# A fused S4 + gated-FFN training step on one core: skip products as diagonal matmuls, more buffers in the transform stages, and stores queued one step later

## The chip, the core and the metric

The kernel runs on one core of one Trainium2 chip. Its time is the device time of an execution in microseconds (us). Six executions had a median of 1852.91 us (1845.04 to 1858.05). Within a core, five engines each work through a queue of their own: TensorE (PE in the profile; its weight loads are PEld), VectorE (DVE), ScalarE (ACT), GpSimd (POOL) and SyncE (SP), which issues most DMA transfers.

Each experiment was timed in five rounds against the kernel before, on the same chip. A ratio is the mean time of one kernel's fast runs over that of the other's of the same rounds, so it is not quite the ratio of the medians that I quote beside it.

## The reference, cut to what matters

The program computes the output of a block and its gradients. `x` is layer-normed to `xn`; an S4 branch (a long convolution done with FFTs, plus a per-channel skip) and a gated feed-forward branch are added; then all is differentiated.

```python
xn = _layernorm(x)
out = x + _A_ref(xn, ...) + _B_ref(xn, ...)
# in _A_ref:   y = irfft(rfft(u) * rfft(K))[:L] + u * Dskip      # u is xn, Dskip has one value per channel
# in _B_ref:   h = relu(x @ W_gate) * (x @ W_up);  return h @ W_down
_out, _vjp = jax.vjp(_f, ...);  grads = _vjp(grad_out)            # L = 2048, D = 576, F = 4608, N = 128
```

So two products with `Dskip` are needed at the very end: `xn * Dskip` for the output, and `grad_out * Dskip` for the gradient that flows back into the layer norm.

## The kernel before

The feed-forward branch goes through F in 12 chunks (0 to 11). Per chunk, an `a_unit` makes hidden activations, `outdx` makes output and input gradient for one tile of 128 rows (summed over chunks in DRAM, `acc_dram`, by a DMA that adds), and `dw_down`, `dw_gu` and `dw_left` make the weight gradients. The S4 branch is interleaved with this: forward transform (`p1`), kernel stage (`p2`), last transform (`p3`), twice, for the two halves of the channels. In chunk 11 the 16 row tiles are finished by `Final`: its terms are added into the same PSUM sum, and VectorE and ScalarE do the rest.

```python
    def fwd1(self, hf, ns, load, ap, n, gap):                 # first step of a transform
        for n2 in range(ST):
            ...
            A = ap.tile([P, 2, ns, DH], BF16, name=f"fA{ns}")     # same pool as the loaded tiles
            ...                                                  # matmul into PSUM, copy into A
            nc.sync.dma_start(self.A[ns][hf][:, n2], A[:])

    def p3(self, hf, n, gap):                                 # second step of the last transform
            fp = self.pool(c, f"p3_f{hf}", 2, "right")
            zp = self.pool(c, f"p3_z{hf}", 3, "right")
            for h in range(ST + 1):
                old, Z = Z, None
                if h < ST:
                    ...                                          # mix: 4 small matmuls, 2 copies
                    Z = self.product(zp, pp, sg[:, 0], sk[:], False), self.product(zp, pp, sg[:, 1], sk[:], True)
                if old is not None:
                    for i in range(2):
                        Ct = fp.tile([P, 2, 1, DH], BF16, name="fC2")
                        yield from self.unmix(Ct[:, :, 0, :], old[i])
                        nc.sync.dma_start(self.mix_in(self.C[2][hf], h - 1)[:, :, i:i + 1, :], Ct[:])

class Final:
    def load(self, t):                                        # two row tiles ahead
        ...
        base = self.pool.tile([P, 2, D], F32, name="f_base")     # self.pool has 3 buffers
        nc.vector.tensor_tensor(base[:], xg[:], self.dsk[:].unsqueeze(1).to_broadcast([P, 2, D]), op=ALU.mult)
    def take(self, t, i, cols, ps):                           # four times per row tile
        base = self.parts[t][5]
        dst = self.o[:, 0, cols] if i == 0 else base[:, 1, cols]
        self.g.nc.vector.tensor_tensor(dst, base[:, i, cols], ps, op=ALU.add)
```

Output tiles of the feed-forward branch, `osx`, have three buffers.

## Time and profile before

The first line of the profile page, busy time, share of the span and number of instructions of each engine:

```profile
PE 1741.8 (94%) x16257; PEld 1179.5 (64%) x16257; DVE 1379.2 (75%) x3223; ACT 1173.7 (63%) x2647; POOL 206.0 (11%) x246
```

PE is the engine to watch: 108 us of the span of 1850.2 are idle on it. The table of stretches (start:end, length, then busy time and instructions of PE, PEld, DVE, ACT, POOL; at the end PE's granted clock, DMA share, GB/s) says where:

```profile
core 0: us, PE busy (x) PEld busy (x) DVE busy (x) ACT busy (x) POOL busy (x), PEclk, DMA share, GB/s
90.00:300.00 210.00, 189.78 (x1450) 119.47 (x1449) 146.64 (x337) 141.50 (x321) 19.16 (x28) 0.95 0.91 291
...
1530.00:1620.00 90.00, 74.77 (x507) 40.96 (x504) 77.87 (x254) 62.79 (x168) 6.90 (x8) 0.96 0.85 236
1620.00:1697.00 77.00, 74.33 (x630) 50.86 (x628) 16.75 (x37) 24.17 (x55) 6.90 (x8) 1.00 0.68 190
1697.00:1812.00 115.00, 102.27 (x801) 71.88 (x799) 93.84 (x208) 49.60 (x96) 0.00 (x0) 0.99 0.68 210
```

In the last transform (1530 to 1620) DVE is busy for 77.87 us beside PE's 74.77; in the final rows (1697 to 1812) it is busy for 93.84 of 115. In the final rows DVE's groups of instructions (line, operation, output<-inputs, shape, count | busy us, mean ns | idle time before them, and what ended it) begin with these:

```profile
L1024 DVE TENSOR_TENSOR f_base<-f_xg,dsk 128x1152 f32<-128x1152 bf16 x13 | 17.6, 1357 | 12.7 <-DMA f_xg<-in_grad_out_dram 12.6
L1043 DVE TENSOR_TENSOR f_base<-f_base,ps_mm 128x288 f32<-128x288 f32 x32 | 14.0, 449 | 3.4 <-PE ps_mm L290 3.4
L1043 DVE TENSOR_TENSOR f_o<-f_base,ps_mm 128x288 bf16<-128x288 f32 x32 | 13.9, 447 | 1.5 <-PE ps_mm L290 1.5
```

The base product costs 1.36 us of work, and DVE also stands idle for 12.7 us in front of it, since it waits for a load. From the list of waits of the whole run (waiter <- releaser: us in total, times, longest):

```profile
PE ps_mm L290 <- ACT osx L67: 14.3, 24, 2.2
...
DVE exs L567 <- DMA ex_dram<-exs: 11.9, 5, 5.4
...
ACT osx L67 <- DMA acc_dram<-osx: 8.4, 4, 3.2
...
DVE osx L61 <- DMA acc_dram<-osx: 3.9, 1, 3.9
```

### The profile page before, as it was taken

Reading aid. Unit: us, or ns where it says so; the run is one execution under the profiler, and the core shown is the slowest. Engines: PE = TensorE matmul, PEld = TensorE weight load, DVE = VectorE, ACT = ScalarE, POOL = GpSimd, SP = SyncE. Lnnn points to the kernel's source line nnn. Section 1 sums busy time; section 2 is a strip of 40 time slices with the busy share of each in tenths; the row PEclk is TensorE's granted clock in tenths of the full one; section 3 lists DMA queues with packets and bytes.
Section 4 is the critical chain, followed back from the end, with each engine's and each line's share of the span. In section 5 each row is a group of like instructions: output and inputs, shape, how many; then the busy total and the mean of one; then the engine's idle time right before and its main releaser. Section 6 shows DMA issues by size and latency. Waiting matters only on the chain. (4 is left out here: it accounts for less than half of the span.)

```text
span 1850.2 us, 41883 instructions
## 1 busy us (share of the span) xinstructions
PE 1741.8 (94%) x16257; PEld 1179.5 (64%) x16257; DVE 1379.2 (75%) x3223; ACT 1173.7 (63%) x2647; POOL 206.0 (11%) x246
## 2 busy tenths in 40 slices
PE   7989989999999999999999999999999998899988
PEld 5655547667566666766666766766766754476656
DVE  7565975686898787787887889889888747923872
ACT  5865855686587488477487567657748736733432
POOL 0200002112012012002102101102201100010000
PEclk9989999999999999999999999999999999999999
DMA  8798988668557566776676856856754879785763
GB/s 285 264 325 292 331 243 264 196 172 232 177 125 203 181 183 168 211 186 146 197 203 137 231 157 154 237 159 122 196 177 93 187 230 259 215 220 163 250 196 100
DMA packets 236411, 373.26 MB, mean 202 GB/s; under 512 B 49202, under 2 KB 153140, under 8 KB 234676
## 3 DMA queue, kind: packets, MB, share of 16 engines
q1 hardware_dynamic: 210244, 304.08, 50.6%
q0 software_dynamic: 24384, 51.92, 18.5%
q10 hardware_dynamic: 1584, 14.60, 2.3%
q8 instruction: 127, 2.08, 0.4%
q14 instruction: 72, 0.59, 0.1%
HBM read 233.08 MB, written 137.43 MB: 200 GB/s over the span
## 5 line engine op out<-in xcount | busy, mean ns | idle before, releaser
L67 ACT CAST osx<-ps_mm 128x288 bf16<-128x288 f32 x684 | 262.0, 422 | 72.7 <-PE ps_mm L290 61.6
L303 POOL DMA_DIRECT2D acc_dram<-osx x160 | 139.4, 875 | 1039.2 <-ACT osx L67 582.2
L290 PE MATMUL ps_mm<-wf,dgT 128*128 128x288 bf16 x1152 | 208.9, 288 | 17.0 <-ACT osx L67 11.9
L343 PEld LDWEIGHTS <-rows 128*128 128x128 bf16 x1536 | 146.0, 98 | 97.5 <-issue 4.6
L290 PE MATMUL ps_mm<-wf,duT 128*128 128x288 bf16 x1152 | 207.0, 288 | 0.0
L290 PE MATMUL ps_mm<-wf,hT 128*128 128x288 bf16 x1152 | 186.4, 289 | 7.7 <-ACT osx L67 2.4
L235 PE MATMUL ps_mm<-xT,wd_158 128*128 128x512 bf16 x720 | 182.4, 379 | 0.7 <-ACT xT L149 0.7
L235 PE MATMUL ps_mm<-gT,wd_160 128*128 128x512 bf16 x705 | 180.3, 382 | 2.0 <-ACT obw L67 2.0
L235 PE MATMUL ps_mm<-xT,wd_159 128*128 128x512 bf16 x720 | 181.5, 380 | 0.5 <-ACT obw L67 0.5
L245 DVE SCALAR_TENSOR_TENSOR upm<-rg,ps_mm 128x512 bf16<-128x512 bf16 x144 | 98.1, 682 | 99.2 <-PE ps_mm L235 71.3
L327 PE MATMUL ps_mm<-rows,hN 128*128 128x144 bf16 x2304 | 156.8, 227 | 0.0
L327 PEld LDWEIGHTS <-hN 128*128 128x128 bf16 x2304 | 147.7, 98 | 7.7 <-issue 5.2
L290 PEld LDWEIGHTS <-dgT 128*128 128x128 bf16 x1152 | 109.7, 98 | 53.5 <-issue 25.3
L343 PE MATMUL ps_mm<-duN,rows 128*128 128x384 bf16 x768 | 138.6, 326 | 0.0
L343 PE MATMUL ps_mm<-dgN,rows 128*128 128x384 bf16 x768 | 136.6, 326 | 0.1
L290 PEld LDWEIGHTS <-hT 128*128 128x128 bf16 x1152 | 107.6, 98 | 41.8 <-issue 12.5
L290 PEld LDWEIGHTS <-duT 128*128 128x128 bf16 x1152 | 113.0, 98 | 31.7 <-issue 2.2
L67 ACT CAST obw<-ps_mm 128x384 bf16<-128x384 f32 x105 | 50.1, 477 | 125.6 <-PE ps_mm L343 93.9
L67 ACT CAST dhb<-ps_mm 128x512 bf16<-128x512 f32 x141 | 83.8, 594 | 66.6 <-PE ps_mm L235 64.9
L901 DVE TENSOR_REDUCE Sm<-pr 128x8 f32<-128x256 f32 x288 | 119.1, 413 | 3.6
L243 ACT ACTIVATE rg<-ps_mm 128x512 bf16<-128x512 f32 x144 | 86.9, 604 | 54.7 <-PE ps_mm L235 53.2
L235 PEld LDWEIGHTS <-wd_159 128*128 128x128 bf16 x720 | 65.6, 98 | 62.5 <-issue 2.7
(2513 smaller groups left out, 3511.4 us busy)
## 6 DMA issues: line engine op xcount, KB each, us to landing
acc_dram<-osx POOLq DMA_DIRECT2D x176, 288.0 KB, 4.7
gT<-in_gT_dram SPq DMA_DIRECT2D x48, 640.0 KB, 6.4
xT<-xT_dram SPq DMA_DIRECT2D x44, 640.0 KB, 6.0
rows<-in_gq_dram SPq DMA_DIRECT2D x48, 576.0 KB, 4.7
wf<-in_Wf_dram ACTq DMA_DIRECT2D x11, 1296.0 KB, 8.7
ex_dram<-exs SPq DMA_DIRECT2D x18, 640.0 KB, 5.8
ex<-ex_dram SPq DMA_DIRECT2D x36, 320.0 KB, 3.3
out_dram<-obw SPq DMA_DIRECT2D x96, 96.0 KB, 2.7
```

The costliest lines, as they stand in the source:

```text
L67: self.nc.scalar.copy(out, in_)
L235: nc.tensor.matmul(ps[:], lhsT=w[:, k, fs], rhs=rhs[:, k, :], start=(k == 0), stop=(k == NK - 1))
L243: nc.scalar.activation(rg[:], ps_g[:], ACT.Relu)
L245: nc.vector.scalar_tensor_tensor(upm[:], rg[:], 0.0, ps_u[:], op0=ALU.is_gt, op1=ALU.mult)
L290: nc.tensor.matmul(ps[:, :DH], lhsT=lt, rhs=rh, start=(i == 0), stop=(i == len(mms) - 1))
L303: nc.gpsimd.dma_start(g.acc_dram[:, t, :, :], o[:], accum_op=ALU.add)
L327: nc.tensor.matmul(ps[:, ft * 144:(ft + 1) * 144], lhsT=self.hN[:, st, ft * P:(ft + 1) * P], rhs=gq[:, st, :], start=(st == 0), stop=(st = ...
L343: nc.tensor.matmul(ps[:, :Fc], lhsT=xs[:, st, 0:P], rhs=src[:, st, :], start=(st == 0), stop=(st == ST - 1))
L901: nc.vector.tensor_reduce(out=Sm[:, vi, s0 + dd:s0 + dd + DG, :], in_=pr[:], op=ALU.add, axis=AX.X)
```

## The change

It intends to take the skip products off VectorE, to let transform steps run further ahead of their stores, and to keep loads from standing in the SP queue behind stores that still wait for data.

```diff
 # 1. Final: skip products on PE. The diagonal 128x128 blocks of Dskip come from the host's layout.
-                    mms = last.terms(t, which, hf) + mms
+                    src0 = self.X[(c, sg)][which]
+                    mms = [... terms ...] + [(src0[:, k, js], last.dsk[:, k, a], b) for k, a, b in last.skip(hf)] + mms
-        base = self.pool.tile([P, 2, D], F32, name="f_base")
-        nc.vector.tensor_tensor(base[:], xg[:], self.dsk[:]...to_broadcast([P, 2, D]), op=ALU.mult)
-        self.g.nc.vector.tensor_tensor(dst, base[:, i, cols], ps, op=ALU.add)
+        if i == 0:
+            self.g.bal.copy(self.o[:, 0, cols], ps, DH)                  # VectorE or ScalarE
+        else:
+            self.g.nc.scalar.activation(self.dx[:, cols], ps, ACT.Copy, accum_out=self.m[:, hf:hf + 1])
 # 2. buffers
-        self.op = pool("ffn_o", 3)
+        self.op = pool("ffn_o", 4)                                       # osx
-            A = ap.tile([P, 2, ns, DH], BF16, name=f"fA{ns}")
+            A = op.tile([P, 2, ns, DH], BF16, name=f"fA{ns}")            # own pool, 2 * n - 2 * (n < 4) buffers
-            fp = self.pool(c, f"p3_f{hf}", 2, "right")                   # the same in p1
-            zp = self.pool(c, f"p3_z{hf}", 3, "right")
+            fp = self.pool(c, f"p3_f{hf}", n, "right")                   # n is 4 for p1(0) and p3(1), else 2
+            zp = self.pool(c, f"p3_z{hf}", n, "right")
 # 3. stores one step later
+class Lag:
+    def put(self, nc, dst, src):
+        self.flush()                                                    # queue the previous store
+        self.q.append((nc, dst, src))
-            nc.sync.dma_start(self.A[ns][hf][:, n2], A[:])
+            lag.put(nc, self.A[ns][hf][:, n2], A[:])                     # also for S and C
 # 4. order in p3: the two products no longer come before the two unmixes
-                    Z = self.product(zp, ...False), self.product(zp, ...True)
+                for i in range(2):
+                    if h > 0:  ... unmix(Z[i]); lag.put(...)
+                    if h < ST: Z[i] = self.product(zp, pp, sg[:, i], sk[:], i == 1)
 # 5. product() uses one scratch tile instead of two; exponent tiles of half the size, 5 buffers instead of 3
-            exp_ = self.pool(c, "par_ex", 3)
+            exp_ = self.pool(c, "par_ex", 5)
```

## The prediction

> **What bounds the kernel.** The matrix engine (PE): the page gives it 1741.8 us busy of a span of 1850.2 (94%); its idle time is 108 us, and removed waits can win no more. The table of stretches puts that at: 13 us in 0-90 (start), 20 in 90-300 (first forward transform beside the parameter stage, clock 0.95), 20 in 300-1000, 17 in 1000-1500, 15 in 1530-1620 (last transform), 13 in 1697-1812 (final outputs), 4.5 in the tail. Two stages have another limit: in 1530-1620 the vector engine (DVE) is busy 77.9 of 90 us; in 1697-1812 it is busy 93.8 of 115 and idles 12.7 more in front of `f_base` (groups of that stretch), mostly for the `f_xg` load.
>
> **Costs and gains by stage.**
> 1. Final outputs. DVE loses 16 `f_base` products of 1.36 us (22 us) and 64 PSUM additions of 0.45 us (29 us). ACT loses 16 copies with sum (0.87 us, 14 us) and gets 32 half-width ones (estimate 0.6 us each, 19 us); 32 PSUM copies of about 0.42 us are shared. PE gains 64 groups of three matmuls. Transposes of 128 columns follow each other every 56 ns (four in 0.22 us in the timeline), so I take 55 ns each, the short ones too: 10.6 us. The Trainium skill ("TensorE: Matmul & The Clock Gate", Back-to-back issue gap) gives about 56 ns as isolated gap and 81 as sustained rate for 128 columns; the trace agrees with the first. All 10.6 us are critical. DVE stops being the limit, PE becomes it: 102.3 us busy now + 10.6 + 2 to 3 idle, against 115. **Net 0 to +2 us**: work moves from an engine that was full to one that then is.
> 2. Last transform. With two buffers ACT waits for `C_ydu` stores to free `fC` (about 11 us in the list of waits) and PE behind it for PSUM (some 10 us). Four buffers and alternating unmix and product remove most. But DVE does the same 73 us of products (0.46 + 2x0.30 + 4x0.30 us, 32 times) and is 87% busy, so less than the idle 15 us comes back: **-8**.
> 3. 90-300. PE waits 7.3 us for `fA` copies, which wait for `A_ug` stores or each other: separate, more buffers remove most, and the clock dips (0.80 in 100-125) go with the gaps. Half-size `exs` tiles cut part of DVE's 12 us of waiting for `ex_dram` stores. The 5.3 us wait for `bC` at the change of phase stays. **-8**.
> 4. Fourth `osx` buffer: PE waits 14.3 us behind ACT's `osx` copies, but only 8.4 + 3.9 us of what holds ACT and DVE there are `acc_dram` stores; the rest is three PSUM buffers. **-4**.
> 5. Late stores. The SP queue's own waits on data to store add up to over 150 us, but PE waits on DMA for about 16 us, 14 of them at start and phase change. Loads are early enough: **-2**.
>
> Sum about -21 us: **1832 us**, 8 in 10 between 1812 and 1850. Faster by over 2%: 0.13; within 2%: 0.85; slower: 0.02.
>
> **What would show it.** PE busy up 10-11 us, PE idle down from 108 to about 77. In the final-output stage PE over 95% busy, DVE under 65%, length within 3 us of before. In the last transform no waits on `C_ydu` stores, DVE over 90% busy. No `fA` waits in 90-300.
>
> **What would make it wrong.** New buffers may change the instruction order on PE, and new in-order stalls may eat the gains (or more idle goes). The short matmuls might cost as much as weight loads (98 ns): +8 us. ACT, with sums in front of PSUM release, might hold PE in the final stage. DVE might not limit the last transform: then -12 there.

## The result, and the profile after

The changed kernel takes 1824.81 us (median of 10 runs, 1821.73 to 1830.56) against 1849.99 us (20 runs). The ratio is 0.986, with a 95% interval of 0.9847 to 0.9874, so about 26 us are gone. The same line of the page, and the first three of the same stretches (fixed times: the last transform's products lie in or close to 1530 to 1620 in both kernels, but the work after it lay up to 28 us later before; the final rows follow below, cut where they begin and end):

```profile
PE 1745.0 (96%) x16449; PEld 1183.9 (65%) x16449; DVE 1353.1 (74%) x3175; ACT 1188.6 (65%) x2716; POOL 205.1 (11%) x246
```

```profile
90.00:300.00 210.00, 191.97 (x1498) 121.44 (x1497) 151.76 (x360) 143.74 (x340) 22.79 (x31) 0.95 0.93 297
...
1530.00:1620.00 90.00, 83.76 (x581) 45.70 (x579) 81.52 (x252) 71.56 (x185) 10.26 (x13) 1.00 0.86 240
1620.00:1697.00 77.00, 77.00 (x685) 54.34 (x683) 22.52 (x50) 24.12 (x56) 2.89 (x4) 1.00 0.64 197
```

PE idle time fell from 108 to 76.5 us (1821.5 - 1745.0), almost exactly as predicted. But 192 matmuls were added, and PE's busy time rose by only 3.2 us. The Trainium skill ("Perfetto Trace Analysis", Identifying the Most-Contended Engine) warns that matmul busy share is not a good measure of how close a kernel is to roofline, because matmuls are pipelined. This trace shows a related fault of it: a matmul of 288 columns is recorded as 0.29 us long but the next one starts 0.12 us later, so every stall adds a piece of pipeline to "busy" and every stall removed takes it away.

So I used another measure, worked out from the trace: the time from the start of one matmul to the start of the next, less the usual spacing for its number of columns (0.0555 us for 128, 0.1215 for 288, 0.2155 for 512, and so on). What remains is time **lost** on PE: waits, and also what a lower granted clock costs. (The measure needs a complete record. These two hold 16257 and 16449 matmuls, as many as the 192 added ask for; those of e1, e2, e4 and e5 lack some 147 each, and I don't use it there.) By this measure the run before lost 141.9 us, the run after 105.2, and the added matmuls cost 8.5 us: 141.9 - 105.2 - 8.5 = 28.2 us, which accounts for the 28.7 us between the two profiled spans.

The stretches below are cut where the work cuts itself, so they hold the same feed-forward work in each kernel. "Rest" is from the first weight gradients of chunk 1 to those of chunk 9, "transform" from there to those of chunk 10, "weights" is the weight-gradient stretch that follows, "final rows" is from the first final row tile to the last weight gradients, and the tail is 40 us in all of them.

```
length in us            start  rest(1-9)  transform  weights  final rows   span of the profiled run
before                  297.4   1177.3     173.6      49.9      111.6      1850.2
after                   293.7   1171.5     160.0      49.9      106.2      1821.5
difference               -3.7     -5.8     -13.6       0.0       -5.4       -28.7
```

The final rows, cut in this way (before, then after, from the table of stretches):

```profile
1698.20:1809.80 111.60, 98.86 (x756) 68.90 (x754) 90.80 (x200) 47.34 (x92) 0.00 (x0) 0.98 0.69 214
1675.10:1781.30 106.20, 104.47 (x948) 76.97 (x946) 57.28 (x135) 59.64 (x147) 0.00 (x0) 1.00 0.76 239
```

VectorE's busy share fell from 81% to 54%, and PE is busy for 98% of the stretch. In it the waits of PE on VectorE, in the kernel before,

```profile
PE pt L264 <- DVE dgT L253: 7.7, 3, 3.6
...
PE ps_mm L290 <- DVE f_o L1043: 3.9, 4, 1.1
```

are gone; what is left in the kernel after is a load:

```profile
PE ps_mm L235 <- DMA gT<-in_gT_dram: 1.5, 2, 1.3
```

PE loses 3.0 us there instead of 16.9. The diagonal matmuls are seen in the timeline of PE (start, duration, instruction, number merged):

```profile
1768.29 0.29 PE L291 MATMUL ps_mm<-f_acc,ident_bf 128*128 128x288 bf16 x1
1768.42 0.29 PE L291 MATMUL ps_mm<-dsk,xT 128*128 128x128 bf16 x3
1768.56 0.53 PE L291 MATMUL ps_mm<-wf,hT 128*128 128x288 bf16 x3
```

The three of them push the next matmul back by 0.14 us (1768.42 to 1768.56), not by their recorded 0.29 us.

The two lists of waits differ in these lines (after):

```profile
DVE exs L582 <- DMA ex_dram<-exs: 16.2, 6, 6.3
...
PE ps_mm L291 <- ACT osx L67: 4.8, 10, 1.5
```

PE's waits behind `osx` copies fell from 14.3 to 4.8 us and no engine waits for an `acc_dram` store any more. The waits on the half-size exponent tiles did not fall. Also no engine waits for a store of the last transform (`C_ydu`), where ACT had waited some 12 us before.

### The profile page after: what moved, and what is told of

Same layout as the page of the kernel before. It is cut to its first block, busy times and chain, and to the rows that moved or that the text cites. A ratio compares the mean times of both kernels' runs of the same rounds, so it can differ in the third digit from the quotient of the medians.

```text
span 1821.5 us, 42302 instructions
## 1 busy us (share of the span) xinstructions
PE 1745.0 (96%) x16449; PEld 1183.9 (65%) x16449; DVE 1353.1 (74%) x3175; ACT 1188.6 (65%) x2716; POOL 205.1 (11%) x246
## 5 line engine op out<-in xcount | busy, mean ns | idle before, releaser
L291 PEld LDWEIGHTS <-hT 128*128 128x128 bf16 x1152 | 104.5, 98 | 37.6 <-issue 7.9
```

Of the source, the lines that this page charges most:

```text
L291: nc.tensor.matmul(ps[:, cs], lhsT=lt, rhs=rh, start=(i == 0), stop=(i == len(mms) - 1))
```

## The experiments

My theory was that the five parts of the change add up, each in its own stretch: buffers give most, the diagonal products a few us in the final rows. The rivals: the late stores do it, or the order in the last transform, or one part is worth something only with another. Twelve kernels ran; all gave correct results. First the sizes, with the profile of each cut as above:

```
                        ratio to before (95%)       start  rest   transf.  weights  final rows
before                  1                           297.4  1177.3  173.6    49.9     111.6
after                   0.9860 (0.9847-0.9874)      293.7  1171.5  160.0    49.9     106.2
one part alone
 e1  final stage only   0.9968 (0.9951-0.9984)      298.0  1176.9  170.2    49.9     105.9
 e5  buffers only       1.0032 (1.0012-1.0052)      295.4  1189.3  163.4    56.4     112.6
 e11 4th osx only       1.0008 (0.9982-1.0034)      298.8  1176.3  161.9    61.5     113.3
 e9  4 final buffers    0.9990 (0.9968-1.0012)      295.6  1177.5  175.7    49.9     108.6
one part undone in after
 e2  stores at once     0.9851 (0.9834-0.9868)      292.2  1171.8  160.9    49.9     106.9
 e3  3 osx buffers      0.9928 (0.9911-0.9946)      293.6  1180.7  165.2    51.7     106.7
 e4  few buffers        0.9888 (0.9869-0.9907)      293.1  1172.4  164.1    49.9     105.4
 e6  old order in p3    0.9893 (0.9875-0.9911)      293.0  1176.9  160.9    49.9     105.9
 e7  big exponent tiles 0.9847 (0.9829-0.9865)      288.0  1175.8  159.8    49.9     106.7
another way for the skip products, on top of after
 e8  folded on DVE      0.9905 (0.9885-0.9925)      293.2  1171.9  159.3    59.2     103.4
 e10 ... 4 buffers      0.9904 (0.9882-0.9927)      295.2  1174.0  159.7    59.6     103.7
 e12 ... mixed          0.9891 (0.9871-0.9911)      290.1  1175.2  159.7    59.0     108.0
```

The stretches are of one profiled run of each kernel, and runs of one kernel differ by several us. The profiled run of e5 took 1859.16 us, while three of its six runs took 1851.6 to 1852.8 and three 1859 to 1861; that of e8 took 1829.09 beside a median of 1834.72; that of e3 is its slowest (1840.53). The ratios tell what a kernel is worth; a difference of two or three us in one stretch is only a hint.

### e1: the final stage alone

Edit: the kernel before, with part 1 of the diff.

> The kernel before with only the new final stage (diagonal products on PE, no base products and additions on DVE). Theory (DVE relief): the stage between the down-weight products of chunk 10 and chunk 11 gets about 5 us shorter as in the changed kernel, all earlier stages stay within 1 to 2 us, so the total is 4 to 7 us lower (about 1844 beside 1850). Rival (the final stage only got shorter because the last transform ended earlier and the loads came earlier): total within 2 us of before, or higher by the 8 us of added matmuls.

Measured: 1843.77 us beside 1850.42. The final rows fell from 111.6 to 105.9 us, as in the changed kernel, with the last transform still at its old place. The rival falls: relief of VectorE in this stretch is worth 5.7 us net of the added matmuls. The transform stretch is 3.4 us shorter too, where I had allowed 1 to 2; the kernel before has its first three base products there, which e1 has not.

### e2: stores at once

```diff
     def put(self, nc, dst, src):
-        self.flush()
-        self.q.append((nc, dst, src))
+        nc.sync.dma_start(dst, src)
```

> The changed kernel with every store queued at once, as before; all buffers as in the changed kernel. Theory (buffers do it, the late stores are worth little): 0 to 3 us slower than the changed kernel. Rival (the late stores do it, since loads no longer stand behind waiting stores in the SP queue): 8 us or more slower.

Measured: 1823.24 us, no slower than the changed kernel. The late stores, one of the three parts in the change's title, are worth nothing measurable here. In the kernel before PE waited on DMA only five times, 16.1 us in all, 14.1 of them at the start and at a change of phase.

### e4: few buffers, with late stores and the new order

```diff
-            fp = self.pool(c, f"p3_f{hf}", n, "right")          # the same in p1
-            zp = self.pool(c, f"p3_z{hf}", n, "right")
+            fp = self.pool(c, f"p3_f{hf}", 2, "right")
+            zp = self.pool(c, f"p3_z{hf}", min(n, 3), "right")
             # fA pools: n buffers instead of 2 * n - 2 * (n < 4)
```

> The changed kernel with the old numbers of buffers in the transform stages (2 for fC, s_k and s_ug, 4 instead of 8 for fA where four loads are ahead), late stores kept. Theory (buffers do it): 9 to 14 us slower than the changed kernel, more than half of it in the chunk with the last transform, and ACT again waits for C_ydu stores there, longer than before since the stores are late. Rival (late stores or the alternating order do it): 0 to 3 us slower.

Measured: 1830.48 us, by the ratios 5 us slower than the changed kernel, 4.1 us of it in the transform stretch. That is between the two expectations: the buffers count for about half of what my theory gave them. The waits of ACT on `C_ydu` stores come back, but as 3.3 us, not as more than before.

### e5: the buffers alone

Edit: part 2 of the diff without the `osx` line (and `zp` at `max(n, 3)`), and part 5's single scratch tile, which made room; everything else as before.

> The kernel before with only the buffers of the transform stages raised (and the second scratch tile of the product dropped, for room); stores at once, old order, three osx buffers, old final stage. Theory (buffers do it): 10 to 14 us faster than before, mostly in the chunk with the last transform, no waits on C_ydu stores. Rival (buffers alone only let the work run ahead until DVE is full, order or late stores are needed): under 5 us faster.

Measured: 1855.98 us, which is **slower** than before by 0.3%. The transform stretch did shrink by 10.2 us and the `C_ydu` waits are gone, just as my theory said. But in the profiled run, one of the slower three, 12 us came back in the middle, and 6.5 us in the weight gradients, a stretch that has no transform work at all. Buffers gave what was expected where they were put, and something else took it away. The second part is explained by e11 below; the first is not (see the end of this section).

### e3: three osx buffers

```diff
-        self.op = pool("ffn_o", 4)
+        self.op = pool("ffn_o", 3)
```

> The changed kernel with three instead of four osx buffers. Theory (the fourth osx buffer removes the waits for acc_dram stores, the longest of them 7 us long right before the weight products of chunk 10): 4 to 8 us slower than the changed kernel. Rival (osx stores are covered anyway, the gain outside the final stage comes from the transform order): within 2 us of the changed kernel.

Measured: 1837.64 us, which by the ratios is 13 us slower than the changed kernel: half of the whole gain, from one digit. 9.2 us are in the middle of the run, 5.2 in the transform stretch. PE's waits behind `osx` copies and the store waits are back, as this list of e3's waits shows:

```profile
PE ps_mm L291 <- ACT osx L67: 11.7, 14, 4.1
...
ACT osx L67 <- DMA acc_dram<-osx: 9.4, 5, 5.4
...
DVE osx L61 <- DMA acc_dram<-osx: 4.6, 1, 4.6
```

### e6: the old order in the last transform

Edit: part 4 of the diff undone, `lag.put` kept.

> The changed kernel with the old order inside the last transform (both products, then both inverse mixes), buffers and late stores as changed. Theory A (the alternating order is what takes the in-order stalls out where the transform runs beside the kernel stage and in the last transform): 6 to 12 us slower than the changed kernel. Theory B (buffers take them out, the order is worth little): 0 to 3 us slower.

Measured: 1829.79 us, by the ratios 6 us slower, at the lower edge of theory A. But the loss is hardly in the last transform (0.9 us). 5.4 us of it are in the middle of the run, and of these only about 1 in the chunks beside which the first half's last transform runs (1010 to 1310 us). The rest comes from stretches in which the edited step hardly runs; that the order of instructions changed there is my guess and not shown. So theory A has its size right but not its place.

### e7: big exponent tiles

Edit: part 5's exponent tiles as before (double size, 3 buffers).

> The changed kernel with the exponent tiles of double size again (three buffers). The prediction credited the half-size tiles with part of the gain before 300 us. Theory now (the waits on ex_dram stores did not fall, 16 us after against 12 before, so they gave nothing): within 2 us of the changed kernel. Rival: 3 us or more slower, all of it by the second chunk.

Measured: 1822.59 us: within noise of the changed kernel. The prediction's guess that half-size tiles help is not borne out. In its profile the start is even 5.7 us shorter and the middle 4.3 us longer; the two cancel.

### e8: a trial of a better version, skip products folded in on VectorE

PE is the limit of the changed final rows, so I took its 192 matmuls away again and let VectorE, now half idle there, put the skip products (in bf16) into a tile that an identity matmul adds anyway.

```diff
-    mms = [... terms ...] + [(src0[:, k, js], last.dsk[:, k, a], b) ...] + mms
+    mms = [... terms ...] + mms
+    def fold(self, n):                                   # called one row tile ahead
+        sk = self.spool.tile([P, 2, D], BF16, name="f_sk")
+        nc.vector.tensor_tensor(sk[:], xg[:], self.dsk[:]...to_broadcast([P, 2, D]), op=ALU.mult)
+        nc.vector.tensor_tensor(acc[:], acc[:], sk[:], op=ALU.add)
```

> A trial of a better version: the changed kernel without the 192 diagonal matmuls; VectorE multiplies xn and g by Dskip in bf16 and adds the result to the tile that an identity matmul adds anyway, one step after its load. VectorE gets about 16 x 1.7 us in the final stage where it is busy 50 of 115 us; PE loses the 8 us of added matmuls (0.55 us per row tile by the timeline). Theory (PE limits the final stage of the changed kernel): 6 to 9 us faster than the changed kernel. Rival (something else limits it, or VectorE in order stalls again on the loads): within 3 us.

Measured: 1834.72 us, 8 us **slower** than the changed kernel by the ratios. The final rows were 2.8 us shorter (103.4), but the weight gradients before them grew from 49.9 to 59.2 us (the profiled run, one of the two fastest, shows 5.9 of the 8 us). This is the stretch that e5 had lengthened too.

### e11: the fourth osx buffer alone

Edit: the kernel before with `pool("ffn_o", 4)`; for room also the single scratch tile, and `zp` at `n`.

> The kernel before with a fourth osx buffer; for room the product's second scratch tile is dropped and the first last-transform half gets two instead of three buffers for its products. Theory (the fourth buffer is the largest single part, since taking it from the changed kernel cost 13 us): 7 to 13 us faster than before, PE's waits on osx copies down from 14 to under 6 us. Rival (it is worth that only together with the other changes): under 4 us faster.

Measured: 1853.24 us: nothing gained. No engine waits for an `acc_dram` store any more, but PE's waits behind `osx` copies fell only from 14.3 to 10.0 us, not to under 6:

```profile
PE ps_mm L290 <- ACT osx L67: 10.0, 17, 3.0
```

Again the transform stretch is 11.7 us shorter, and again the weight-gradient stretch is longer, by 11.6 us. Here is VectorE at the start of that stretch (timeline of e11; in brackets the idle time before an instruction and what ended it):

```profile
1636.43 0.46 DVE L61 CAST osx<-ps_mm 128x288 bf16<-128x288 f32 x1 [0.64 <-PE ps_mm L290]
1649.33 1.36 DVE L1023 TENSOR_TENSOR f_base<-f_xg,dsk 128x1152 f32<-128x1152 bf16 x1 [12.44 <-DMA f_xg<-in_grad_out_dram]
1650.60 0.60 DVE L61 CAST obd<-ps_mm 128x432 bf16<-128x432 f32 x1
...
1662.65 1.36 DVE L1023 TENSOR_TENSOR f_base<-f_xg,dsk 128x1152 f32<-128x1152 bf16 x1 [5.68 <-DMA f_xg<-in_grad_out_dram]
1663.93 0.68 DVE L245 SCALAR_TENSOR_TENSOR upm<-rg,ps_mm 128x512 bf16<-128x512 bf16 x1
```

The base product of the first final row tile stands in VectorE's queue in the middle of the weight gradients and waits 12.44 us for its load. SyncE had issued that load at 1631.31 (line 1019 in its timeline), 18.0 us before the product could start; in the kernel before the same took 6.6 us (1505.68 to 1512.30). The DMA share is 1.04 from 1630 to 1649 us, and 0.79 in the kernel before from 1500 to 1516, so here the load was late because the DMA engines were full, as far as the shares tell. The copy that would free PE's PSUM bank (`obd`) stands behind the product, and PE stops:

```profile
PE ps_mm L327 <- DVE obd L61: 5.1, 1, 5.1
...
PE ps_mm L343 <- DVE upm L245: 2.5, 1, 2.5
```

That is a full stop in a stretch that had been loss-free, and it is paid for twice, as the table of stretches for e11 shows:

```profile
1648.50:1655.30 6.80, 4.04 (x35) 4.04 (x35) 3.24 (x3) 0.00 (x0) 0.00 (x0) 0.50 0.92 304
1665.50:1668.90 3.40, 3.40 (x12) 1.59 (x11) 0.24 (x1) 0.00 (x0) 0.00 (x0) 0.50 0.00 0
```

PE's granted clock was 0.50 in these two pieces, during and after the first stop and after the second; it was 1.00 in the whole of this stretch in the kernel before and in the changed one. My estimate from these lines: half of the 4.0 us of work after 1651.3 and half of the 3.4 us, 3.7 us in all, which with the two stops (7.6 us) makes up the 11.6. (In e5, e8 and e10 too the clock is at 0.50 for 6 to 7 us of the weight gradients.) The Trainium skill ("TensorE: Matmul & The Clock Gate", Architectural detail: the array is 16× 32×32, not 1× 128×128) says that ACT and DVE are strict FIFO; this trace agrees, with 12.44 us of it. In the kernel before, the same instruction stood much earlier, and no wait of PE from 1505 to 1530 us is put down to VectorE:

```profile
1512.30 1.36 DVE L1024 TENSOR_TENSOR f_base<-f_xg,dsk 128x1152 f32<-128x1152 bf16 x1 [3.92 <-DMA f_xg<-in_grad_out_dram]
1514.47 1.36 DVE L1024 TENSOR_TENSOR f_base<-f_xg,dsk 128x1152 f32<-128x1152 bf16 x1 [0.82 <-DMA f_xg<-in_grad_out_dram]
```

(The queue order is set when the program is built, and the traces show that it is not the order of the source: this product runs 186 us before the first final row.) The same happened in e5 (three waits on `f_xg`, together 16.2 us in that stretch) and in e8 and e10 (12.7 and 12.9 us at the first product). These four kernels, and e12 below, have a weight-gradient stretch of 56.4 to 61.5 us. Every kernel with the diagonal matmuls for all row tiles has 49.9 to 51.7 us, and so have the two whose first base products stand before that stretch (the kernel before, and e9).

So the diagonal products have a second worth that e1 cannot show: they leave no instruction in VectorE's queue that waits for the final stage's first loads. Of the kernels that ran, only those with them for all row tiles, or with the base products earlier, keep the weight gradients at 50 to 52 us. The parts of the change do not add up, and measured alone (e5, e11) two of them looked worthless.

### e9: four buffers in the old final stage

```diff
-            self.pool = pool("fin3", 3)
+            self.pool = pool("fin3", 4)
```

> The kernel before with one change: four instead of three buffers for the tiles of the final stage, still loaded two row tiles ahead, so that a load no longer needs the buffers of the row tile just finished. VectorE keeps all its work (91 us in a stage of 112). Theory A (VectorE's work limits the stage, as the prediction says): at most 3 us faster than before. Theory B (VectorE stands in order behind the base product that waits for its f_xg load, 12.6 us, and that stall is what limits the stage): the wait for f_xg falls under 4 us, the stage loses 8 us or more and the kernel is 6 to 12 us faster.

Measured: 1848.66 us, no change that is clear. Its final rows are 3.0 us shorter and the transform stretch 2.1 longer. In that stretch now stand the first three base products, at 1620 to 1634 us, each with a wait of 4 to 6 us for `f_xg`. And in the final rows the experiment did not do what it was built for, since the wait stayed:

```profile
DVE f_base L1024 <- DMA f_xg<-in_grad_out_dram: 11.2, 9, 2.1
```

The list of the SP queue's own waits in e9's final rows points to why a buffer doesn't help:

```profile
SPq L1052 <- DVE f_base L1043: 29.1, 12, 4.4
```

The SP queue waits 29.1 us in front of the store of the output (line 1052), whose data VectorE has not made yet, and loads of a later tile stand behind that store. It also waits 13.3 us in front of loads of `xt` whose buffer PE still reads, so data not yet made is not all that holds the queue. So e9 cannot tell whether VectorE's work or its in-order wait limited the old final rows.

### e10 and e12: two more tries at the fold

e10 is e8 with `pool("fin3", 4)`.

> The trial e8 (skip products folded into the accumulator on VectorE, no diagonal matmuls) with four instead of three buffers in the final stage. In e8 VectorE stood 14 us in front of the product that waits for f_xg, and PE lost 16 us in that chunk, though VectorE was busy only 75 of 112 us. Theory (the in-order stall on the load is the cause): the wait goes under 4 us, PE loses under 4 us in the last chunk, and the kernel is 6 to 9 us faster than the changed kernel (about 1816). Rival (VectorE's chain itself is too long): within 3 us of e8.

Measured: 1833.31 us, as e8. VectorE waited for `f_xg` 38 us in all, of which the first waits are in the weight gradients (timeline of VectorE in e10):

```profile
1641.66 0.76 DVE L1064 TENSOR_TENSOR f_sk<-f_xg,dsk 128x1152 bf16<-128x1152 bf16 x1 [12.90 <-DMA f_xg<-in_grad_out_dram]
```

The expected numbers were missed (the waits did not go). Its final rows (table of stretches) have VectorE at 69.81 of 103.60 us:

```profile
1688.50:1792.10 103.60, 97.25 (x755) 68.26 (x752) 69.81 (x149) 63.48 (x157) 0.00 (x0) 1.00 0.70 218
```

By the measure of lost time PE still loses 8.9 us there, against 3.0 in the changed kernel. VectorE is only two thirds busy, so its amount of work can hardly be the cause; its waits in order are the likely one.

e12 keeps the diagonal matmuls for the first four row tiles, loads three tiles ahead with five buffers, and moves the output stores to GpSimd's queue.

```diff
-                mms = ... + [... last.skip(hf)] + mms
+                mms = ... + ([... last.skip(hf)] if t < 4 else []) + mms
-            self.pool = pool("fin3", 3)
+            self.pool = pool("fin3", 5)                  # loads; work tiles have a pool of 3
-        for n in range(t, min(t + 3, ST)):
+        for n in range(t, min(t + 4, ST)):
-        nc.sync.dma_start(g.out0_v[:, t, :], o[:, 0, :])     # out1 likewise
+        nc.gpsimd.dma_start(g.out0_v[:, t, :], o[:, 0, :])
```

> A second trial of a better version. The first four row tiles keep the diagonal matmuls, so that no VectorE instruction waits for the first loads of the final stage (12.9 and 5.4 us waits in e10, in the weight products of chunk 10); the other twelve fold the skip products into the accumulator on VectorE. Loaded tiles have five buffers and are loaded three row tiles ahead, and the output stores go to GpSimd's queue, so that loads no longer stand behind stores that wait for their data. Theory (what ate the gain in e8 and e10 were VectorE's in-order waits for f_xg, caused by the order in the SP queue and not by VectorE's work): VectorE's waits for f_xg fall from 38 us to under 6 us, PE loses under 4 us in the last chunk, the kernel is 4 to 7 us faster than the changed kernel (1818 to 1821). Rival (VectorE's work itself, about 75 us in 112, holds PE): as slow as e8, 1833.

Measured: 1832.35 us, and I had expected 1818 to 1821. VectorE's wait for `f_xg` fell from 38 to 18 us (I had expected under 6), but PE now stops in the weight gradients for other reasons (waits of e12 there):

```profile
PE ps_mm L345 <- DMA rows<-xs_dram: 3.6, 1, 3.6
PE ps_mm L236 <- DVE obw L62: 3.3, 1, 3.3
```

and among VectorE's waits:

```profile
DVE obw L62 <- DMA out_dram<-obw: 16.5, 1, 16.5
```

VectorE stands idle for 16.5 us before a copy into a weight-gradient tile (`obw`), until an earlier store has left its buffer. The timeline of SyncE shows that store late: ScalarE had written its data by 1647.4 us, but it was issued at 1654.12, with six loads for the final rows issued in between (`f_acc`, `S`, two of `bC`, `xt`, `f_xg`), and the copy started at 1658.40. The load of `rows` that PE waited for was issued at 1640.42, after SyncE had stood 5.6 us in front of a `bC` load. By this order, loads of the final rows now hold up in the SP queue what the weight gradients need; a run with fewer of them ahead would test it and was not made. The final rows are no better than in e10 either (108.0 us, of which PE loses 11.1). None of the three trials beats the changed kernel, and it remains the fastest that this study knows, together with e2 and e7, which can't be told from it.

### What stays open

- Why the base products moved from 1512 us to 1620 us in e9 and into the weight gradients in e5 and e11. It happened in kernels in which the buffers of the final stage, or of what runs before it, were given more SBUF. That the space for the final stage's tiles then comes free later is my guess and was not tested by itself.
- Why e5 lost 12 us in the middle of its profiled run (8.2 of them from 1034 to 1345 us, beside the last transform of the first half), while e11 lost nothing there. Both have the single scratch tile; e5 has the new `fA` pools, e11 doesn't.
- Whether VectorE's work or its in-order wait limited the old final rows. e9 could not take the wait away.
- What gives the 5.8 us in the middle of the run. Undoing the fourth `osx` buffer or the order costs that much there, but the fourth buffer alone (e11) brings only 1 us.

## Why the prediction was right or wrong

It said 1832 us, between 1812 and 1850, and within 2%; 1824.81 was measured, and the ratio is within 2%. The gain was 26 us where 21 were predicted. The sum came close while its terms did not: two were too small and two too large, and that they made up for each other is luck.

1. **Final outputs, "net 0 to +2 us": wrong, -5.4.** Two terms were mis-sized. The added matmuls cost 8.5 us, not 10.6: the three matmuls with 128, 128 and 32 columns, or 96, 128 and 64, follow each other after 56, 42 or 28 ns by their width, and I had taken 55 ns for all. The Trainium skill ("TensorE: Matmul & The Clock Gate", Back-to-back issue gap) has about 25 ns as the floor up to 64 columns, which this trace comes close to (28 ns here, and 25 ns in its long streams of 32 columns), and I should have used it. The larger error is "102.3 us busy now" as PE's work: busy time contains the pipeline of every stalled matmul. By spacing, PE lost 16.9 us in the final rows where idle time shows some 13, and 3.0 remained. That VectorE would stop being the limit and PE become it was right (PE 104.5 of 106.2 us busy, DVE 57.3).
2. **Last transform, -8: -13.6 in that stretch,** but it holds the `osx` effect too. Undoing the buffers costs 4.1 us there, undoing the fourth `osx` buffer 5.2, undoing the order 0.9; e1, with the final stage alone, is 3.4 us shorter there. In the fixed stretch of 1530 to 1620 us PE's idle time fell from 15.2 to 6.2 us, which is near the 8 that I meant. The `C_ydu` waits went and DVE is 91% busy (81.5 of 90), as said.
3. **90-300, -8: -3.7 by the weight gradients of chunk 1.** `fA` waits fell from 7.3 to 2.9 us, not to zero; the clock there stayed at 0.95, and the exponent tiles gave nothing (e7).
4. **Fourth `osx` buffer, -4: undoing it costs 13 us, and alone it gives nothing.** As to PE's waits the split into stores and PSUM buffers was nearly right: with the fourth buffer alone (e11) no wait for `acc_dram` stores was left, and PE's waits behind `osx` copies fell by 4.3 us, from 14.3 to 10.0. The step that failed is to add this term to the others: in the changed kernel the same waits are 4.8 us, and 11.7 when the buffer is taken away again (e3), so the buffer and the other parts work together. How 6.9 us of these waits become 13 us of time is not shown. The Trainium skill ("Perfetto Trace Analysis", Optimization Strategy) notes that the same gap coming back over a stretch can mean too few buffers; the 24 short waits on one tile name, none longer than 2.2 us, were that only in part, since 17 of them stayed in e11.
5. **Late stores, -2: nothing** (e2), for the reason given there.

"PE busy up 10-11 us" was wrong (+3.2); idle of about 77 us was right (76.5). I had named new in-order stalls as a risk, but not that the parts depend on each other: without the diagonal products the time won by buffers is lost again to an in-order wait.

## What to carry to other kernels

Before adding buffers, ask what will stand in each in-order queue at the moment the time saved becomes free; an instruction that waits for a load is harmless where there is slack and stops everything behind it where there is none, so look at where it lands after the change, not only at its length. A part of a change that gives nothing alone may be worth half the gain beside another part, so undo parts from the changed kernel as well as adding them to the old one. And measure a pipelined engine by the spacing of its instructions, not by its busy time.

## What the Trainium skill lacked or had wrong

- "TensorE: Matmul & The Clock Gate", Back-to-back issue gap: it gives 81 ns (128 columns) and 131 ns (512) as sustained spacing of pairs of weight load and matmul. In this case's dense stream, each matmul with its own weights, the median spacing is 56 ns and 216 ns, which are its figures for the isolated gap; 288 columns take 122 ns, and in the diagonal products 32 or 64 columns take 28 ns.
- "Perfetto Trace Analysis", Identifying the Most-Contended Engine: beside matmul busy share, which it rightly calls a bad measure, it offers two totals over a window and nothing that shows single stalls. Here 8.5 us of added matmul work showed as 3.2 us of busy time, and PE's loss in the final rows was 16.9 us by spacing where idle time showed about 13.
- No page that I read says what a DMA wait inside an engine's strict FIFO costs the other engines. Here one VectorE product waiting 12.44 us for its load, and two more behind it, lengthened a loss-free stretch from 49.9 to 61.5 us: 7.6 us of stops of PE, and most of the rest in 10.2 us at a granted clock of 0.50.
- Nor did I find a number for what a store queued before its data is ready costs the loads behind it in the SP queue: in e9 SP waited 29.1 us in front of one line's stores, and a fourth buffer left VectorE's waits for the load behind them at 11.2 us (12.6 before).
